# Two value products per unit put into one slot: third and fourth chunk in slot 5 instead of slots 4 and 6

## The chip, the cores and the metric

The kernel runs on one core of a Trainium2 chip. The metric is the time of one execution on the device in microseconds (us). A measurement shows the median of several runs; the profile is of one execution.

The engines named below are TensorE (PE in rows; PEld is its weight load), VectorE (DVE), ScalarE (ACT), GpSimd (POOL) and SyncE (SP), which issues most of the transfers. Each works through its own list of instructions in order and waits on the others only through semaphores.

## What is computed

The first half is attention with normalised queries and keys, the second a mixture of eight experts, of which each token takes one:

```python
q_n, k_n = rmsnorm(q, g_q), rmsnorm(k, g_k)        # (8, 12, 448, 64)
scores = scale * np.matmul(q_n, k_n.transpose(0, 1, 3, 2))
scores = scores - np.max(scores, axis=-1, keepdims=True)
attn = np.exp(scores)
attn = attn / (np.sum(attn, axis=-1, keepdims=True) + 1e-09)
x = np.matmul(attn, v)                             # to (3584, 768)
...
logits = x @ w_gate + modality_bias[modality_id]
e_idx = np.argmax(logits, axis=1)
...
h = np.maximum(x[mask] @ w1[e], 0.0)               # per expert e
out[mask] = gate_w[mask, None] * (h @ w2[e])
```

The change lies in the attention half.

## The kernel before

The 8 batches of 12 heads are worked through in 48 units (`NU`); a unit is two heads of one batch. The 448 positions of each of the two heads are cut into chunks of 128 rows, with one chunk (number 3) that is shared: it holds 64 rows of either head. So a unit has seven row chunks, and the loop gives it seven slots (`NJ = 7`); slot number n = 7 * unit + j is what the table `PLAN` speaks in.

In slot j of unit i the loop issues:

- `st(i, j)`, L1000: the transposed scores of one chunk, two products of 448 columns into PSUM (four in slot 3), and, on ScalarE, the exponential of them into the buffer `p` of the unit. PSUM has two such buffers, so st of a slot needs the exponential of two slots before.
- `sa(u, j)`, L972 and L967: the scores of a unit two further on, the other way round, from which VectorE takes the maximum per row. There are two PSUM buffers here as well: sa of a slot needs the maximum of two slots before to be done.
- what `PLAN` puts there: the transposes of queries and keys (`tr`, slots 0 and 3), of the row maxima (`mt`, slot 1), of the attention output (`xt`, slot 4), the column sums (`sums`, L1054, slot 2 of every second unit), the gate products (`gates`, L1061, slot 6 of every fourth), the matmuls of routing (`rt`, slot 6 of some).
- the value products `av(u, c)`, L1039, of the unit before, u = i - 1, with c from 0 to 3:

```python
for h in range(2):
    j, r = (3, (LO, HI)[h]) if c == 3 else (4 * h + c, slice(0, 128))
    PE.matmul(t["av"][64 * h : 64 * h + 64, :S], lhsT=vv[r, u % 3, j],
              rhs=t["p"][r, j], start=c == 0, stop=c == 3)
```

Chunks 0 to 2 multiply 128 rows by 64 columns for either head; chunk 3 multiplies 64 rows by 64 columns. All four add up in one PSUM tile, of which there is one (`ps_o`). When chunk 3 has been issued, ScalarE copies the tile out with the next slot's first work (`avcopy`), so that chunk 0 of the next unit may begin.

`PLAN['av']` gives the slot of each of the four chunks: `AVJ[c]` in

```python
put(NJ * (u + 1) + (AVJ[c] if u < NU - 2 else min(AVJ[c], 6)), "av", u, c)
...
if c == 3:
    at(pre["A"] if j else post, n + (j > 0), lambda u=u: avcopy(u))
```

Further on, work of routing (small steps of VectorE, GpSimd and ScalarE that decide each token's expert) is mixed into the slots from a queue, a step or two per slot. When the loop ends, the four chunks of the last unit are issued in a row, and the expert half begins.

Of the kernel before, what the change touches and what calls it, by code (L numbers as in the profile page):

```python
# [30 lines left out]
NT1 = NB1 * S  # L31
BIG = float(1 << 20)
ET = mybir.EngineType
PLAN = {'rtj': 6, 'rushat': 36, 'av': (1, 1, 4, 6), 'xt': 4, 'xte': (2, 5), 'sm': 2, 'la': 6, 'rc': 9, 'csv': (1,), 'csj': (3, 6), 'csd': (1, 1), 'cse': (2, 1), 'sa': 14, 'mt': 6, 'tk': 21, 'tq': 18, 'nq': 26, 'nk': 26, 'sk': 49, 'sq': 50, 'rs': 48, 'ld': 58, 'first': {('sq', 0): -22, ('sk', 0): -21, ('nk', 0): -20, ('nq', 0): -18, ('sq', 1): -19, ('sk', 1): -19, ('sq', 2): -18, ('sk', 2): -18, ('nk', 1): -16, ('nq', 1): -13, ('tk', 0): -18, ('tq', 0): -17, ('sa', 0): -15, ('tk', 1): -13, ('tq', 1): -11, ('sa', 1): -5, ('mt', 0): -8, ('tk', 2): -8, ('tq', 2): -3, ('nq', 2): -8, ('nk', 2): -14, ('nq', 3): 3, ('nk', 3): -3, ('sq', 3): -13, ('sk', 3): -13, ('sq', 4): -8, ('sk', 4): -15, ('sq', 6): -2, ('sk', 6): 6, ('sk', 7): 11, ('sq', 8): 5, ('sk', 8): 5, ('nk', 7): 20, ('nq', 9): 31, ('tq', 3): 5, ('mt', 1): 2, ('nq', 5): 6, ('mt', 8): 50, ('rs', 0): -20, ('rs', 2): -16, ('nq', 8): 35, ('rs', 5): -7, ('mt', 2): 8, ('nq', 7): 25, ('mt', 5): 30, ('sk', 9): 15, ('tk', 9): 43, ('mt', 6): 37, ('nq', 6): 17, ('sa', 5): 23, ('rs', 7): 16, ('rs', 8): 30, ('mt', 4): 23, ('nk', 4): -2, ('ld', 9): 6, ('tk', 5): 16, ('sk', 5): -9, ('tk', 3): 0, ('tk', 4): 8, ('nk', 5): 0, ('sq', 5): -15, ('mt', 3): 16, ('nq', 4): 1, ('sa', 4): 16, ('tq', 4): 12, ('sa', 3): 9, ('sa', 2): 1, ('tq', 5): 19, ('mt', 7): 45, ('tq', 7): 31, ('sa', 7): 37, ('nk', 6): 16, ('tq', 6): 24, ('sq', 7): 12, ('tk', 6): 21, ('sa', 6): 30, ('tk', 7): 28}, 'rs0': {0: 0, 2: 1, 5: 0, 7: 0, 8: 2}, 'sastep': 1, 'start': -22, 'warm': {-22: 19, -21: 3, -20: 1, -16: 4, -15: 1, -13: 5, -10: 2, -7: 3, -6: 1, -5: 1, 5: 1, 7: 1}, 'warmn': 1, 'early': 1, 'late0': 1, 'pmp0': 2, 'ramp': 10, 'pmp': (0, 0, 1, 1, 1, 0, 1), 'nv': [(0, 0)], 'pmpa': (1, 0, 1, 0, 1, 1, 1), 'rush': (1, 1, 1), 'ps': [(6, 1), (4, 0), (3, 0), (2, 0)], 'pa': [], 'rtr': 6, 'sml': 4, 'lv': (-10, 0), 'lg': 16, 'lz': 13, 'gc': 24, 's1': (1, 4)}
MANUAL = {ET.PE, ET.DVE, ET.Activation, ET.Pool, ET.SP}
IOFF = bass.IndirectOffsetOnAxis

# [29 lines left out]
def kernel(  # L67
# [727 lines left out]
    if True:  # L795
# [27 lines left out]
        def sumsq(u, i):  # L823
# [4 lines left out]
            sq = sq_b[i]  # L828
            if (u, i) in PLAN["pa"]:
                x = T[u][nm].rearrange("p h c d -> p (h c) d")  # L830
# [9 lines left out]
            def reduce():  # L840
                if (u, i) in PLAN["ps"]:
                    o = t["ss"][:, i, 8 * j : 8 * j + 8].unsqueeze(2)
                    w = D // 2
                    while w:
                        G.tensor_tensor(out=sq[:, :, 0:w] if w > 1 else o, in0=sq[:, :, 0:w],
                                        in1=sq[:, :, w : 2 * w], op=ALU.add)
                        w //= 2
                    return
                V.tensor_reduce(
                    out=t["ss"][:, i, 8 * j : 8 * j + 8], in_=sq, op=ALU.add, axis=AX.X  # L850
                )
# [35 lines left out]
        def tr(u, g):  # L887
# [32 lines left out]

            own = u < PLAN["early"]
            x = ps if own else h_.bitcast(F32)
# [38 lines left out]
        def sa(u, j):  # L961
# [6 lines left out]
            else:  # L968
                h = j // 4
                a = 128 * j - h * S  # L970
                r = slice(0, 128) if u >= PLAN["early"] else (LO, HI)[h]
                PE.matmul(ps[:, :S], lhsT=t["qq"][r, h, a : a + 128], rhs=t["kk"][h][r], start=True, stop=True)  # L972
# [234 lines left out]
        man = ExitStack()  # L1207
        P = PLAN
        man.enter_context(tc.manual_schedule(engines=MANUAL))
# [50 lines left out]
        post, fin = {}, {}  # L1260
        P = PLAN
        CSV, CSJ, CSD, CSE = (P[x] for x in ("csv", "csj", "csd", "cse"))
# [384 lines left out]
```

## Time and profile before

| | |
|---|---|
| median of 3 runs | 1071.11 us (1068.9 to 1071.33) |
| the profiled execution | 1071.33 us |
| its span, first to last instruction | 1069.3 us |
| TensorE busy | 1040.7 us, 97% of the span |
| VectorE busy | 779.2 us, 73% |
| ScalarE busy | 696.2 us, 65% |
| GpSimd busy | 710.3 us, 66% |
| mean granted clock of TensorE | 0.993 |

The table is an average over two halves with different work; the attention loop ends at about 568 us. A share of busy time says which engine has the least room, and not whether its instructions follow each other as closely as they could. That is read from start to start in the timeline.

### The profile page before, as it was taken

What the parts mean: (1) busy time and instruction counts of PE and PEld (TensorE: products, weight loads), DVE (VectorE), ACT (ScalarE), POOL (GpSimd) and SP (SyncE); (2) the same over time, 40 slices, a digit from 0 to 9 for tenths busy, and PEclk for the clock granted to TensorE, in tenths of its full rate; (3) what the DMA queues carried; (4) which work ended last, traced back from release to release, by engine and by line L of the source; (5) the groups of instructions that cost most, each with busy time, mean ns of one, the idle gap of its engine ahead of it and who ended that gap; (6) DMA issues with size and microseconds to landing.
All of it is one profiled execution on the core that took longest, in us unless ns stands there. A gap on an engine that the chain in (4) does not pass through costs nothing.

```text
span 1069.3 us, 19016 instructions
## 1 busy us (share of the span) xinstructions
PE 1040.7 (97%) x6536; PEld 804.7 (75%) x6536; DVE 779.2 (73%) x1337; ACT 696.2 (65%) x1293; POOL 710.3 (66%) x740
## 2 busy tenths in 40 slices
PE   8899999999999999998999999999999999999995
PEld 7555555555555555554557999999999999999995
DVE  5767788998889888898778895856765668556740
ACT  6887888878888788887664654555554555445531
POOL 7788777787877878788875647555445564555451
PEclk9999999999999999999999999999999999999998
DMA  7866767867778678765675704344283432334261
GB/s 188 196 155 147 165 147 188 184 146 162 152 178 188 151 160 155 176 157 118 160 220 188 176 31 118 105 119 115 85 300 93 120 104 76 74 104 119 70 210 50
DMA packets 151800, 153.72 MB, mean 144 GB/s; under 512 B 73530, under 2 KB 141582, under 8 KB 151184
## 3 DMA queue, kind: packets, MB, share of 16 engines
q1 hardware_dynamic: 126340, 110.59, 43.4%
q0 software_dynamic: 25328, 41.82, 12.5%
q8 instruction: 54, 0.88, 0.4%
q14 instruction: 50, 0.41, 0.2%
q10 hardware_dynamic: 28, 0.01, 0.0%
HBM read 150.31 MB, written 33.39 MB: 172 GB/s over the span
## 4 chain that ended last, share of the span: by engine, by line
PE 82%; DVE 5%; POOL 4%; issue 4%; DMA 3%; ACT 2%; SPq 0%; POOLq 0%; DVEq 0%; ACTq 0%
PE ph L591 21%; PE py L621 20%; PE av L1039 12%; PE st L1000 12%; PE sa L972 5%; PE tr L895 3%; PE xt L1096 2%; PE sm L1054 2%; DVE at_hlw L52 2%; POOL r2w L52 1%; PE warm L1249 1%; PE sm L1061 1%; PE mt L983 1%; DVE xw L52 1%; PE sa L967 1%
## 5 line engine op out<-in xcount | busy, mean ns | idle before, releaser
L591 PE MATMUL ph<-xw,w1w 128*128 128x256 f32 x2016 | 246.5, 283 | 1.0 <-ACT xw L52 0.6
L591 PEld LDWEIGHTS ph<-xw,w1w 128*128 128x128 f32 x2016 | 244.0, 192 | 3.4 <-issue 1.4
L52 DVE TENSOR_REDUCE at_hlw<-sa 128x1 f32<-128x448 f32 x336 | 205.6, 617 | 36.4 <-PE sa L972 17.2
L1000 PE MATMUL st<-w1w 128*128 128x448 f32 (+1 forms) x480 | 175.8, 416 | 0.6 <-ACT r2w L52 0.6
L52 ACT ACTIVATE r2w<-st 128x448 f32<-128x448 f32 x168 | 90.8, 543 | 53.2 <-PE st L1000 44.3
L52 POOL TENSOR_TENSOR r2w<-r2w 128x448 f32<-128x448 f32 (+1 forms) x72 | 82.2, 1142 | 63.0 <-ACT at_w2lw L52 22.6
L1000 PEld LDWEIGHTS st<-w1w 128*128 128x128 f32 (+1 forms) x480 | 84.9, 191 | 45.0 <-ACT r2w L52 17.8
L52 POOL DMA_INDIRECT r<-in_moe_w_dram,tb_w x60 | 79.5, 1324 | 58.1 <-DVE w1w L52 42.8
L972 PE MATMUL sa<-w1w 128*128 128x448 f32 (+1 forms) x288 | 110.1, 383 | 8.1 <-DVE at_hlw L52 4.0
L621 PE MATMUL py<-w2lw,hhw 128*128 128x384 f32 x448 | 113.7, 334 | 0.0
L52 ACT ACTIVATE hhw<-ph 128x512 fp32r<-128x512 f32 x56 | 33.5, 598 | 120.6 <-PE ph L591 100.7
L52 DVE TENSOR_TENSOR w1w<-r,w1w 128x768 fp32r<-128x768 f32 x112 | 103.7, 954 | 8.4 <-ACT w1w L52 7.2
L52 ACT CAST w1w<-xw 64x448 fp32r<-64x448 f32 x188 | 105.5, 561 | 3.6 <-issue 1.6
L52 DVE TENSOR_TENSOR w2lw<-r2w,w2ha 128x1536 fp32r<-128x1536 f32 x28 | 49.1, 1757 | 79.1 <-ACT w2ha L52 42.1
L52 POOL DMA_INDIRECT r2w<-in_moe_w_dram,tb_vi x48 | 50.9, 1059 | 83.5 <-DVE w2lw L52 71.6
L52 ACT ACTIVATE at_w2lw<-st 128x448 f32<-128x448 f32 x168 | 90.4, 543 | 23.8 <-PE st L1000 16.8
L1000 PE MATMUL st<-w1w,w2ha 65*128 65x448 f32 x288 | 100.8, 370 | 0.3 <-DMA w1w<-xw 0.3
L52 POOL TENSOR_TENSOR xrw<-r,at_hlw 112x512 f32<-112x512 f32 x95 | 98.1, 1053 | 0.6
L52 ACT CAST w1w<-r 128x768 fp32r<-128x768 f32 x112 | 95.2, 905 | 0.0
L621 PEld LDWEIGHTS py<-w2lw,hhw 128*128 128x128 f32 x448 | 80.9, 188 | 0.0
L52 ACT ACTIVATE yw<-py,ltn 128x384 f32<-128x384 f32 x55 | 29.3, 578 | 77.0 <-PE py L621 48.8
L52 POOL TENSOR_TENSOR r2w<-r2w,at_w2lw 64x448 f32<-64x448 f32 (+1 forms) x48 | 55.0, 1146 | 27.0 <-DVE r2w L52 14.7
(315 smaller groups left out, 2227.1 us busy)
## 6 DMA issues: line engine op xcount, KB each, us to landing
w1w<-xw SPq DMA_DIRECT2D x312, 112.0 KB
xg<-xrw SPq DMA_DIRECT2D x14, 768.0 KB
xrw<-xg SPq DMA_DIRECT2D x56, 192.0 KB
r<-in_q_dram SPq DMA_DIRECT2D x19, 448.0 KB
r<-in_k_dram SPq DMA_DIRECT2D x19, 448.0 KB
w2ha<-xw SPq DMA_DIRECT2D x72, 112.0 KB
r2w<-in_v_dram SPq DMA_DIRECT2D x24, 224.0 KB
at_w2lw<-in_v_dram SPq DMA_DIRECT2D x24, 224.0 KB
```

Of the source, the lines that this page charges most:

```text
L52: return fn(*a, **kw)
L591: PE.matmul(ps[:, i], lhsT=lt_, rhs=rt_[:, c], start=n == 0, stop=n == 17)
L621: PE.matmul(ps[n][:, :384], lhsT=lt_[:, j, 128 * t : 128 * t + 128], rhs=rt_[:, 384 * n : 384 * n + 384], start=j == 0 and m == 0, stop=j ...
L895: PE.transpose(sp[:, c], src[:, c], idn[:CP, :CP])
L967: PE.matmul(ps[:, :S], lhsT=qm_b[u % 2], rhs=hi_b[u % 2][1], start=True, stop=True)
L972: PE.matmul(ps[:, :S], lhsT=t["qq"][r, h, a : a + 128], rhs=t["kk"][h][r], start=True, stop=True)
L983: PE.transpose(ps[0:NJ, :128], t["mx"], idn)
L1000: PE.matmul(ps[:, :S], lhsT=l, rhs=t["qq"][:, h] if first else t["ql"][:, h], start=first and (j != 3 or h == 0), stop=not first and (j != ...
L1039: PE.matmul(t["av"][64 * h : 64 * h + 64, :S], lhsT=vv[r, u % 3, j], rhs=t["p"][r, j], start=c == 0, stop=c == 3)
L1054: PE.matmul(R[g][32 * i : 32 * i + 32, :S], lhsT=sel[:, m], rhs=T[u + i // 2]["cs"][:, i % 2], start=m == 0, stop=False, tile_position=(0, ...
L1061: PE.matmul(sm[32 * i : 32 * i + 32, :S], lhsT=wg[:, (4 * g + i) % NP], rhs=T[4 * g + i]["xt"], start=False, stop=True, tile_position=(0, ...
L1096: PE.transpose(ps[:CP, 128 * c : 128 * c + 128], T[u]["xt"][:, c * CP : (c + 1) * CP], idn)
```

## The change

One entry of the table is changed, the slots of the four value chunks:

```diff
 PLAN = {
 ...
-'av': (1, 1, 4, 6),
+'av': (1, 1, 5, 5),
 ...
```

No instruction is added or removed. On TensorE, in the slots 4 to 6 of an ordinary unit, stood before (a number ending a name is that of the tile; `st_4` is the score tile of slot 4; x2 and x4 are matmuls alike in a row):

```order
L972 MATMUL sa_4_1486<-w1w 128x448
L1039 MATMUL av_1435<-at_w2lw,r2w 64x448 x2
L1096 MATMUL xt_1490<-idn,at_hlw 112x128 x4
L1000 MATMUL st_5_1506<-w1w 128x448
L1000 MATMUL st_5_1506<-w1w,w2ha 128x448
L972 MATMUL sa_5_1509<-w1w 128x448
L1000 MATMUL st_6_1518<-w1w 128x448
L1000 MATMUL st_6_1518<-w1w,w2ha 128x448
L972 MATMUL sa_6_1521<-w1w 128x448
L1039 MATMUL av_1435<-at_w2lw,r2w 64x448 x2
L1000 MATMUL st_0_1530<-w1w 128x448
```

and in the same place stands now:

```order
L972 MATMUL sa_4_1486<-w1w 128x448
L1096 MATMUL xt_1488<-idn,at_hlw 112x128 x4
L1000 MATMUL st_5_1504<-w1w 128x448
L1000 MATMUL st_5_1504<-w1w,w2ha 128x448
L972 MATMUL sa_5_1507<-w1w 128x448
L1039 MATMUL av_1435<-at_w2lw,r2w 64x448 x4
L1000 MATMUL st_6_1520<-w1w 128x448
L1000 MATMUL st_6_1520<-w1w,w2ha 128x448
L972 MATMUL sa_6_1523<-w1w 128x448
L1000 MATMUL st_0_1531<-w1w 128x448
```

The two pairs of value products have moved together behind sa of slot 5; xt follows sa of slot 4 directly, and st of the next unit's slot 0 follows sa of slot 6.

On ScalarE the copy of the value tile goes along. From the exponential of slot 5 to that of the next unit's slot 0 (`xrw<-r` is a square of queries for their norm) stood before, at another unit:

```order
L52 ACTIVATE r2w<-st_5_1023 128x448
L52 ACTIVATE r2w<-st_6_1033 128x448
L52 ACTIVATE xrw<-r_0_152 112x512
L52 COPY at_w2lw<-av_942 128x448
L52 ACTIVATE at_w2lw<-st_0_1045 128x448
```

and now:

```order
L52 ACTIVATE r2w<-st_5_1021 128x448
L52 COPY at_w2lw<-av_942 128x448
L52 ACTIVATE r2w<-st_6_1035 128x448
L52 ACTIVATE xrw<-r_0_152 112x512
L52 ACTIVATE at_w2lw<-st_0_1046 128x448
```

The copy has moved ahead of the exponential of slot 6 and of the square. On VectorE, GpSimd and SyncE the instructions stand in the same order as before.

## Rows read from the trace of the kernel before

**Rows 1.** Windows: length, then busy us of PE, PEld, DVE, ACT, POOL, PEclk, DMA.

```profile
100.00:488.00 388.00, 385.23 (x2088) 221.07 (x2085) 329.00 (x648) 318.96 (x700) 301.39 (x323) 1.00 0.72 163
488.00:515.00 27.00, 24.14 (x122) 12.61 (x120) 24.07 (x55) 15.96 (x35) 21.59 (x29) 0.94 0.48 111
```

**Rows 2.** Timeline of PE, slots 4 to 6 of a unit: start us, us.

```profile
214.24 0.37 PE L972 MATMUL sa<-w1w 128*128 128x448 f32 x1
...
215.44 0.65 PE L1096 MATMUL xt<-idn,at_hhw 128*112 128x128 f32 x4
215.84 0.45 PE L1000 MATMUL st<-w1w 128*128 128x448 f32 x1
...
216.34 0.37 PE L972 MATMUL sa<-w1w 128*128 128x448 f32 x1
...
216.75 0.37 PE L1000 MATMUL st<-w1w,w2ha 65*128 65x448 f32 x1
216.96 0.37 PE L972 MATMUL sa<-w1w 128*128 128x448 f32 x1
217.26 0.97 PE L1039 MATMUL av<-at_w2lw 64*64 64x448 f32 x4
218.16 0.47 PE L1000 MATMUL st<-w1w 128*128 128x448 f32 x1
218.47 0.37 PE L1000 MATMUL st<-w1w,w2ha 65*128 65x448 f32 x1
```

**Rows 3.** Timeline of PE, late unit: xt behind st, no value chunk ahead.

```profile
549.32 0.37 PE L1000 MATMUL st<-w1w,w2ha 65*128 65x448 f32 x1
549.53 0.60 PE L1096 MATMUL xt<-idn,at_hhw 128*112 128x128 f32 x4
549.88 0.64 PE L1000 MATMUL st<-w1w 128*128 128x448 f32 x2
```

**Rows 4.** Timeline of PE: two value chunks in a row, and four.

```profile
219.99 1.72 PE L1039 MATMUL av<-r2w,at_w2lw 128*64 128x448 f32 x8
221.65 0.28 PE L983 MATMUL mt<-idn,at_hlw 128*7 128x128 f32 x1
...
568.14 3.38 PE L1039 MATMUL av<-at_w2lw 128*64 128x448 f32 x16
571.44 0.74 PE L591 MATMUL ph<-xw,w1w 128*128 128x256 f32 x4
```

**Rows 5.** Waits of PE from 40 to 488 us: total, times, longest.

```profile
PE av L1039 <- ACT at_hhw L52: 1.3, 2, 0.9
```

**Rows 6.** Timeline of DVE from slot 5 on, first and last of three units.

```profile
151.48 1.25 DVE L52 TENSOR_REDUCE at_hlw<-sa 128x1 f32<-128x448 f32 x2
152.65 0.89 DVE L53 TENSOR_REDUCE lo<-at_hlw 112x32 f32<-112x384 f32 x1
...
157.12 0.61 DVE L52 TENSOR_REDUCE at_hlw<-sa 128x1 f32<-128x448 f32 x1
...
420.68 0.89 DVE L53 TENSOR_REDUCE lo<-at_hlw 112x32 f32<-112x384 f32 x1
```

**Rows 7.** Timeline of PE: sa of slot 3 in the first of these units.

```profile
157.94 0.37 PE L967 MATMUL sa<-xw,w2ha 128*128 128x448 f32 x1
```

**Rows 8.** Timeline of DVE, a unit with gates and routing: first and last named.

```profile
217.91 1.47 DVE L52 SCALAR_TENSOR_TENSOR r2w<-r2w,half 128x448 f32<-128x448 f32 x1
...
227.08 0.61 DVE L52 TENSOR_REDUCE at_hlw<-sa 128x1 f32<-128x448 f32 x1
```

**Rows 9.** Timeline of PE in the same unit: sa of slot 5, gate products.

```profile
227.74 0.47 PE L972 MATMUL sa<-w1w 128*128 128x448 f32 x1 [0.39 <-DVE at_hlw L52]
...
230.10 0.56 PE L1061 MATMUL sm<-at_hlw,wg 128*32 128x448 f32 x1
```

**Rows 10.** Timeline of POOL: the last addition of a unit's half-sums.

```profile
389.88 1.14 POOL L52 TENSOR_TENSOR at_w2lw<-r2w,at_w2lw 128x448 f32<-128x448 f32 x1
```

**Rows 11.** Timeline of PE: the column sums that read it.

```profile
391.89 0.57 PE L1054 MATMUL sm<-at_hhw,sel 128*32 128x448 f32 x2
```

More of the change, by code (lines that the diff above doesn't have):

```diff
@@ L33 @@
 ET = mybir.EngineType
-PLAN = {'rtj': 6, 'rushat': 36, 'av': (1, 1, 4, 6), 'xt': 4, 'xte': (2, 5), 'sm': 2, 'la': 6, 'rc': 9, 'csv': (1,), 'csj': (3, 6), 'csd': (1, 1), 'cse': (2, 1), 'sa': 14, 'mt': 6, 'tk': 21, 'tq': 18, 'nq': 26, 'nk': 26, 'sk': 49, 'sq': 50, 'rs': 48, 'ld': 58, 'first': {('sq', 0): -22, ('sk', 0): -21, ('nk', 0): -20, ('nq', 0): -18, ('sq', 1): -19, ('sk', 1): -19, ('sq', 2): -18, ('sk', 2): -18, ('nk', 1): -16, ('nq', 1): -13, ('tk', 0): -18, ('tq', 0): -17, ('sa', 0): -15, ('tk', 1): -13, ('tq', 1): -11, ('sa', 1): -5, ('mt', 0): -8, ('tk', 2): -8, ('tq', 2): -3, ('nq', 2): -8, ('nk', 2): -14, ('nq', 3): 3, ('nk', 3): -3, ('sq', 3): -13, ('sk', 3): -13, ('sq', 4): -8, ('sk', 4): -15, ('sq', 6): -2, ('sk', 6): 6, ('sk', 7): 11, ('sq', 8): 5, ('sk', 8): 5, ('nk', 7): 20, ('nq', 9): 31, ('tq', 3): 5, ('mt', 1): 2, ('nq', 5): 6, ('mt', 8): 50, ('rs', 0): -20, ('rs', 2): -16, ('nq', 8): 35, ('rs', 5): -7, ('mt', 2): 8, ('nq', 7): 25, ('mt', 5): 30, ('sk', 9): 15, ('tk', 9): 43, ('mt', 6): 37, ('nq', 6): 17, ('sa', 5): 23, ('rs', 7): 16, ('rs', 8): 30, ('mt', 4): 23, ('nk', 4): -2, ('ld', 9): 6, ('tk', 5): 16, ('sk', 5): -9, ('tk', 3): 0, ('tk', 4): 8, ('nk', 5): 0, ('sq', 5): -15, ('mt', 3): 16, ('nq', 4): 1, ('sa', 4): 16, ('tq', 4): 12, ('sa', 3): 9, ('sa', 2): 1, ('tq', 5): 19, ('mt', 7): 45, ('tq', 7): 31, ('sa', 7): 37, ('nk', 6): 16, ('tq', 6): 24, ('sq', 7): 12, ('tk', 6): 21, ('sa', 6): 30, ('tk', 7): 28}, 'rs0': {0: 0, 2: 1, 5: 0, 7: 0, 8: 2}, 'sastep': 1, 'start': -22, 'warm': {-22: 19, -21: 3, -20: 1, -16: 4, -15: 1, -13: 5, -10: 2, -7: 3, -6: 1, -5: 1, 5: 1, 7: 1}, 'warmn': 1, 'early': 1, 'late0': 1, 'pmp0': 2, 'ramp': 10, 'pmp': (0, 0, 1, 1, 1, 0, 1), 'nv': [(0, 0)], 'pmpa': (1, 0, 1, 0, 1, 1, 1), 'rush': (1, 1, 1), 'ps': [(6, 1), (4, 0), (3, 0), (2, 0)], 'pa': [], 'rtr': 6, 'sml': 4, 'lv': (-10, 0), 'lg': 16, 'lz': 13, 'gc': 24, 's1': (1, 4)}
@@ new lines @@
+PLAN = {'rtj': 6, 'rushat': 36, 'av': (1, 1, 5, 5), 'xt': 4, 'xte': (2, 5), 'sm': 2, 'la': 6, 'rc': 9, 'csv': (1,), 'csj': (3, 6), 'csd': (1, 1), 'cse': (2, 1), 'sa': 14, 'mt': 6, 'tk': 21, 'tq': 18, 'nq': 26, 'nk': 26, 'sk': 49, 'sq': 50, 'rs': 48, 'ld': 58, 'first': {('sq', 0): -22, ('sk', 0): -21, ('nk', 0): -20, ('nq', 0): -18, ('sq', 1): -19, ('sk', 1): -19, ('sq', 2): -18, ('sk', 2): -18, ('nk', 1): -16, ('nq', 1): -13, ('tk', 0): -18, ('tq', 0): -17, ('sa', 0): -15, ('tk', 1): -13, ('tq', 1): -11, ('sa', 1): -5, ('mt', 0): -8, ('tk', 2): -8, ('tq', 2): -3, ('nq', 2): -8, ('nk', 2): -14, ('nq', 3): 3, ('nk', 3): -3, ('sq', 3): -13, ('sk', 3): -13, ('sq', 4): -8, ('sk', 4): -15, ('sq', 6): -2, ('sk', 6): 6, ('sk', 7): 11, ('sq', 8): 5, ('sk', 8): 5, ('nk', 7): 20, ('nq', 9): 31, ('tq', 3): 5, ('mt', 1): 2, ('nq', 5): 6, ('mt', 8): 50, ('rs', 0): -20, ('rs', 2): -16, ('nq', 8): 35, ('rs', 5): -7, ('mt', 2): 8, ('nq', 7): 25, ('mt', 5): 30, ('sk', 9): 15, ('tk', 9): 43, ('mt', 6): 37, ('nq', 6): 17, ('sa', 5): 23, ('rs', 7): 16, ('rs', 8): 30, ('mt', 4): 23, ('nk', 4): -2, ('ld', 9): 6, ('tk', 5): 16, ('sk', 5): -9, ('tk', 3): 0, ('tk', 4): 8, ('nk', 5): 0, ('sq', 5): -15, ('mt', 3): 16, ('nq', 4): 1, ('sa', 4): 16, ('tq', 4): 12, ('sa', 3): 9, ('sa', 2): 1, ('tq', 5): 19, ('mt', 7): 45, ('tq', 7): 31, ('sa', 7): 37, ('nk', 6): 16, ('tq', 6): 24, ('sq', 7): 12, ('tk', 6): 21, ('sa', 6): 30, ('tk', 7): 28}, 'rs0': {0: 0, 2: 1, 5: 0, 7: 0, 8: 2}, 'sastep': 1, 'start': -22, 'warm': {-22: 19, -21: 3, -20: 1, -16: 4, -15: 1, -13: 5, -10: 2, -7: 3, -6: 1, -5: 1, 5: 1, 7: 1}, 'warmn': 1, 'early': 1, 'late0': 1, 'pmp0': 2, 'ramp': 10, 'pmp': (0, 0, 1, 1, 1, 0, 1), 'nv': [(0, 0)], 'pmpa': (1, 0, 1, 0, 1, 1, 1), 'rush': (1, 1, 1), 'ps': [(6, 1), (4, 0), (3, 0), (2, 0)], 'pa': [], 'rtr': 6, 'sml': 4, 'lv': (-10, 0), 'lg': 16, 'lz': 13, 'gc': 24, 's1': (1, 4)}
```

## The prediction

> **What bounds the kernel now.** The table of windows comes first [rows 1]. Between 100 and 488 us, where 35 of the 48 units run, TensorE's matmuls fill 385.23 of 388 us at the full granted clock; VectorE is busy for 329.00 us (85%), so it is the engine that is next. Only in 488 to 515 us does this turn round: VectorE 24.07 of 27 us, TensorE 24.14, the granted clock 0.94. So in most of the loop a change is worth what it changes in TensorE's own sequence, as long as VectorE and ScalarE can still follow.
>
> Busy time can hide a delay between matmuls, so the timeline of one unit is read next, by the distances from start to start [rows 2]. Shown are slots 4 to 6 of an ordinary unit. Matmuls of one kind follow each other at 0.20 to 0.21 us (216.75 to 216.96). A value product (av) after sa starts at 0.30 (216.96 to 217.26); what follows a value chunk starts 0.90 after it (217.26 to 218.16), and the second st after it 0.31 later (218.16 to 218.47) where it is otherwise 0.20. So there is a toll for going into the narrow value products and one for coming out.
>
> **The change part by part: TensorE.** Work is neither added nor removed; the sum is of tolls.
>
> Slot 4 now: from sa to the first st of slot 5 takes 1.60 (214.24 to 215.84), of it 0.40 for the transposes xt (215.44 to 215.84). Without the value chunk, xt follows directly. That occurs once in the trace [rows 3]: 0.21 to get into xt and 0.35 until the next st. So slot 4 will take 0.56, which is 1.04 less.
>
> Slot 6 now: from sa to the second st of the next slot is 1.51 (216.96 to 218.47). Later it will be as from slot 5 to 6 now, 0.41 (216.34 to 216.75). 1.10 less.
>
> Slot 5 now: 0.41. Later: 0.30 into the chunks, the pair, then 0.31. The pair's cost is the question. Two chunks in a row in slot 1 take 1.66 (219.99 to 221.65) [rows 4], so that a second one costs 0.76; by this row the pair takes 1.66. But chunks 0 to 2 are products of 128 rows by 64 columns of the array, and chunk 3 is 64 by 64. The last unit's four chunks in a row take 3.30 (568.14 to 571.44) [rows 4]: three of one shape are 0.90 + 0.76 + 0.76 = 2.42, which leaves 0.88, a full price within rounding, for the fourth. I take this row, since it holds the very pair: 0.90 + 0.90 = 1.80. The Trainium skill, "TensorEngine Tiling (Array Packing)", section Tiling Modes, says that changing the tiling mode, and not just the tile, drains TensorE. The trace agrees: the fourth chunk costs 0.12 us more than one of the same shape. By the rule the pair saves nothing in itself.
>
> By the row of slot 1 alone the gain in an ordinary unit would be 0.28 us, by the row of the last unit it is 0.14, as follows.
>
> Slot 5 will take 0.30 + 1.80 + 0.31 = 2.41, which is 2.00 more. An ordinary unit: -1.04 - 1.10 + 2.00 = -0.14 us; what is left is one toll on the way in (0.09) and the 0.05 by which xt is shorter. There are 22 such units: -3.1. In the others slot 4 or slot 6 has more work of the narrow kind behind the chunk, so its tolls stay and only the chunk's 0.90 goes: 8 units with gate products in slot 6, -1.04 - 0.90 + 2.00 = +0.06 each, +0.5; 6 units with sums in slot 4, -0.90 - 1.10 + 2.00 = 0. In 4 units routing products of the wide kind follow in slot 6, which keep the 0.31 behind them: -1.04 - (0.30 + 0.90 - 0.21 + 0.05) + 2.00 = -0.08, -0.3. The first units have no xt: in four of them slot 4 gives 1.10 as well, -0.2 each, -0.8, of which I count half, since TensorE also waits for others there. The last two give -0.2. Together -3.5.
>
> **ScalarE.** Its one moved step is the copy of av out of PSUM. It now stands before the exponential of slot 6, not behind it. TensorE waited 1.3 us, twice, at av for that copy, in the early units [rows 5]. These waits go, less what the sums behind them then wait for: -0.8. The price: ScalarE is in order, so the exponential of slot 6 is held until av is done. But its own input comes after av on TensorE, so it loses only the copy. I cost this at nothing. The cover is slot 0: the st of slot 1 is the next that needs that exponential, and between lie two st, one sa and four transposes, some 0.6 + 0.35 us by the rows of their kinds [rows 2, 3]. Were the cover gone, that st would be late by up to the length of the copy in each unit.
>
> **VectorE, where the loss lies.** The order on VectorE, GpSimd and the DMA queues is the same before and after. But TensorE's slots change in length. sa of slot 5 comes 1.04 earlier; sa of slot 6 comes later by -1.04 + (0.30 + 1.80) - 0.21 + (0.31 - 0.20) = +0.96, I use 0.94 for the rounding; what follows in slot 0 is 0.15 earlier again. VectorE's maximum over sa of slot 6 moves with it, by 0.94, where VectorE does not lag, and all behind it (the half-sums, the sums of squares, the maximum of slot 0) has 0.94 + 0.15 = 1.09 less time until TensorE wants the buffer back: sa of slot 3 needs the maximum of slot 1. In an ordinary unit VectorE has idle time in slots 0 to 3 that takes this up. In units in which routing work is mixed in it has none:
>
> - Three units are like [rows 6]: from 151.48 VectorE runs on without a gap, through two routing steps (0.89 the first), to the maximum at 157.12, done 157.73. TensorE starts sa of slot 3 at 157.94 [rows 7], so 0.21 are in hand. After: done 158.67, wanted at 157.79: a wait of 0.88. The last of the three, at 420.68, reads the same; the middle one has 0.2 more in hand. Together 2.5.
> - Two units are like [rows 8]: VectorE runs without a gap from 217.91, and a routing step delays it again before the maximum of slot 3 (227.08 to 227.61). Today sa of slot 5 waits for that (227.74) and the chunk of slot 6 is done when the gate sums start at 230.10 [rows 9]. After: the maximum is done at 228.55 and sa starts at 228.68; then 0.30 + 1.80 + 0.31 + 0.21 to sa of slot 6 and 0.30 to the sums: 231.60, 1.5 later. Together about 3.1, with what the unit would have given.
> - Four units, in which VectorE now lags by more than 0.8 when slot 6 ends, hand on TensorE's earlier start only as a wait: 0.5 in all, an estimate.
>
> **GpSimd.** It adds the half-sums up from VectorE's step behind the maximum of slot 6, so it too is 0.94 late. In every second unit the column sums of slot 2 need it: 391.02 against 391.89 [rows 10, 11], 0.87 in hand, 1.09 needed: 0.3 with the signal; two others have just enough, 0.1 each. 0.5.
>
> What is not in the trace is whether VectorE's small steps change in length when they fall beside other work of GpSimd; they run from 0.17 to over 2 us. I bound the waits by this: none of them comes (0), or as much again comes in the routing units (13); I take the sum above, 6.6, since each term is read from its own rows.
>
> **The sum.** -3.5 - 0.8 + 6.6 = +2.3 us, on the profiled execution's 1071.33, of which 1069.3 is its span: 1073.6. That execution lies 0.2 above the median, so 1073.4 is to be compared with it; I put it at 1073. At the two ends of the waits the same sum gives 1066.8 and 1080.
>
> **The rivals.**
> 1. *The waits don't come*, because VectorE makes the 0.94 good. Then -3.5 - 0.8 = -4.3: about 1066.8. For it: VectorE has 59 us idle in 388 [rows 1], 1.7 per unit, more than 0.94. Against: in the five units named its rows have no gap.
> 2. *VectorE and ScalarE fall behind in ordinary units too.* The place is sa of slot 3 after a short slot 2. There the trace has some 0.8 in hand in the tightest units without sums, of which ScalarE's later copy takes about 0.3. It decides from 0.5 more per unit; each 0.3 beyond that costs 22 x 0.3 = 6.6, so 1073 + 6 = 1079. For it: three short slots, 6, 0 and 2, now lie around one long one. Against: VectorE's gaps there. This ends slower.
> 3. *The shape change is not paid*, the pair at 1.66: 40 x 0.14 = 5.6 less, 1067.4. Against it stands the row of four chunks.
> 4. *The stretch at 488 to 515 decides.* There TensorE waits for VectorE, which waits for GpSimd, and the clock fell; if that wait shortens or lengthens by 2 us, the time moves by 2 to 4 us either way: 1069 to 1077. The order there is unchanged, so I expect the same stall.
>
> **How the numbers follow.** The sum as worked out 0.54, the first rival 0.17, the second 0.13, the third 0.03, the fourth 0.13. 0.3% of 1071.11 is 3.2 us, about what a measurement can tell: faster is below 1067.9, slower above 1074.3. My own case by itself reaches from 1070.5 to 1075.5, so it gives 0.36 same and 0.18 slower; rivals 1 and 3 are faster but for 0.02; rival 2 is slower; rival 4 is split 0.07 same, 0.02 faster, 0.04 slower. Together faster 0.20, same 0.45, slower 0.35. For 8 in 10 the range takes in rival 1 down to its own value and leaves out the far part of rival 2: 1066.8 to 1077.5.
>
> **What the profile after would show.** av in slot 5 as one group of eight records with 1.80 from its start to st 6, not 1.66; ordinary units 0.14 shorter; no wait of av for ScalarE's copy; waits of sa of slot 3 for VectorE of 0.8 or more near 158, 292 and 426 us, and a longer unit near 218 and 353; VectorE idle about 1.4 us before the maximum of slot 6 in ordinary units. I am wrong if the waits of sa for VectorE stay at some 2 us between 100 and 488, or if they appear in ordinary units as well.

## The result and the profile after

The changed kernel takes 1076.92 us (median of 15 runs, 1073.05 to 1081.97), the kernel before 1071.40 in the same session (15 runs, 1068.89 to 1075.15): a ratio of 1.0053, 95% interval 1.0037 to 1.0069, so 4.0 to 7.4 us slower. The forecast was 1073, its range 1066.8 to 1077.5. The profiled execution is the longest of its 15, 1081.97 us with a span of 1080.0, while the profile of before (1071.33) lies close to its median. So it has to be read unit by unit, and what only this execution met has to be told apart.

The table of windows, with the columns of [rows 1]:

```profile
100.00:488.00 388.00, 377.71 (x2043) 219.04 (x2043) 317.28 (x631) 310.29 (x687) 296.10 (x314) 0.99 0.72 162
488.00:515.00 27.00, 25.91 (x139) 14.40 (x136) 24.25 (x58) 18.84 (x43) 20.98 (x30) 1.00 0.52 120
```

TensorE has 7.5 us less busy time in the long stretch (377.71 for 385.23). The short one, rival 4's place, can't be compared so: the changed kernel is 9.8 us behind by then and does other work in it. It is judged by its units further on. The timeline of TensorE in slots 4 to 6 of a unit, against [rows 2]:

```profile
272.80 0.37 PE L972 MATMUL sa<-w1w 128*128 128x448 f32 x1
273.00 0.60 PE L1096 MATMUL xt<-idn,at_hhw 128*112 128x128 f32 x4
273.36 0.45 PE L1000 MATMUL st<-w1w 128*128 128x448 f32 x1
273.64 0.37 PE L1000 MATMUL st<-w1w,w2ha 65*128 65x448 f32 x1
273.86 0.37 PE L972 MATMUL sa<-w1w 128*128 128x448 f32 x1
274.16 1.87 PE L1039 MATMUL av<-r2w 128*64 128x448 f32 x8
275.96 0.47 PE L1000 MATMUL st<-w1w 128*128 128x448 f32 x1
276.27 0.37 PE L1000 MATMUL st<-w1w,w2ha 65*128 65x448 f32 x1
276.48 0.37 PE L972 MATMUL sa<-w1w 128*128 128x448 f32 x1
```

The pair costs 1.80 from its start to the next st (274.16 to 275.96), the toll behind it is 0.31, and slot 4 is down to 0.56 (272.80 to 273.36). VectorE idles ahead of the maximum of slot 6, as forecast:

```profile
276.89 0.62 DVE L52 TENSOR_REDUCE at_hlw<-sa 128x1 f32<-128x448 f32 x1 [1.47 <-PE sa L972]
```

Waits of TensorE from 40 to 500 us: total, times, longest. No wait of av for ScalarE's copy is left, against [rows 5]:

```profile
PE sa L972 <- DVE at_hlw L52: 5.8, 7, 1.4
PE mt L983 <- DVE at_hlw L52: 3.1, 3, 2.0
PE st L1000 <- DMA w1w<-xw: 3.0, 1, 3.0
PE sa L967 <- DVE at_hlw L52: 1.7, 4, 0.4
```

L967 is sa of slot 3. Before, the two lines of sa had 1.7 and 0.9. Of the 5.8, one wait of 1.34 is put down to VectorE wrongly:

```profile
279.70 0.44 PE L972 MATMUL sa<-w1w 128*128 128x448 f32 x1 [1.34 <-DVE at_hlw L52]
```

VectorE's last maximum ahead of it, the one at 276.89 shown above, was done by 277.51. What came just before the start is the end of a copy into w1w: it was issued at 273.35, and the last of its 16 completions in the trace stands at 279.61. So the waits at sa of L972 for VectorE are 4.5 us, and this one belongs to the late transfers below.

A finer measure serves for all that follows: the start of sa of slot 0 in each unit, here less the same start before. From one unit to the next this difference moves by -0.15 or -0.16 in ordinary units and by 0.08 in units with gates. It moves by about +0.9 in five units with routing (those that begin at 153, 219, 288, 353 and 421 us before; 0.80 at 288, and the last measured as 0.91 where only the later units are changed, since here a late transfer lies on it). VectorE in the first of these, against [rows 6]:

```profile
155.35 0.62 DVE L52 TENSOR_REDUCE at_hlw<-sa 128x1 f32<-128x448 f32 x1 [1.47 <-PE sa L972]
155.90 0.90 DVE L53 TENSOR_REDUCE lo<-at_hlw 112x32 f32<-112x384 f32 x1
...
157.87 0.84 DVE L53 TENSOR_TENSOR lo<-lo,ball 112x32 f32<-112x32 f32 x1
158.64 0.61 DVE L52 TENSOR_REDUCE at_hlw<-sa 128x1 f32<-128x448 f32 x1
...
160.36 0.61 DVE L52 TENSOR_REDUCE at_hlw<-sa 128x1 f32<-128x448 f32 x1
```

It first waits 1.47 for sa of slot 6, then runs two routing steps without a gap. TensorE pays for it in two places: by the starts against before, 0.26 at sa of slot 2 and the rest, 0.68, at sa of slot 3 [rows 7]:

```profile
159.31 0.47 PE L972 MATMUL sa<-w1w 128*128 128x448 f32 x1
...
161.02 0.47 PE L967 MATMUL sa<-xw,w2ha 128*128 128x448 f32 x1 [0.44 <-DVE at_hlw L52]
```

Two things were not foreseen. The first is an early unit (it begins at 67 us), in which mt waits 1.96 for VectorE, where it waited 0.92 before, and the granted clock then stands at the lower of its two levels (1.2 GHz, half) from 69.31 to 72.73. The unit is 2.36 longer. First before, then after:

```profile
68.52 0.28 PE L983 MATMUL mt<-idn,at_hlw 128*7 128x128 f32 x1 [0.92 <-DVE at_hlw L52]
```
```profile
67.14 0.37 PE L972 MATMUL sa<-w1w 128*128 128x448 f32 x1
69.47 0.38 PE L983 MATMUL mt<-idn,at_hlw 128*7 128x128 f32 x1 [1.96 <-DVE at_hlw L52]
69.50 1.84 PE L1000 MATMUL st<-w1w 128*128 128x448 f32 x4
```

The second are late transfers: copies of queries and keys from one half of the partitions to the other (w1w from xw, 112 KB each). The longest:

```profile
429.48 0.47 PE L1000 MATMUL st<-w1w 65*128 65x448 f32 x1 [2.97 <-DMA w1w<-xw]
```

This wait and the one at 279.70 were each followed by another fall of the granted clock to half, at 431.13 and 280.94.

### The profile page after: what moved, and what is told of

Same layout as the page of the kernel before. It is cut to its first block, busy times and chain, and to the rows that moved or that the text cites. A ratio compares the mean times of both kernels' runs of the same rounds, so it can differ in the third digit from the quotient of the medians.

```text
span 1080.0 us, 19016 instructions
## 1 busy us (share of the span) xinstructions
PE 1042.0 (96%) x6536; PEld 808.5 (75%) x6536; DVE 773.3 (72%) x1337; ACT 694.4 (64%) x1293; POOL 704.1 (65%) x740
## 4 chain that ended last, share of the span: by engine, by line
PE 76%; DVE 7%; DMA 6%; issue 5%; POOL 3%; ACT 3%; SPq 0%; POOLq 0%; DVEq 0%; ACTq 0%
PE ph L591 20%; PE py L621 18%; PE av L1039 12%; PE st L1000 12%; PE sa L972 4%; DMA w1w<-xw 3%; PE tr L895 3%; DVE at_hlw L52 3%; PE sm L1054 2%; PE xt L1096 1%; PE warm L1249 1%; DVE xw L52 1%; POOL r2w L52 1%; PE sa L967 1%; ACT xw L52 1%
## 5 line engine op out<-in xcount | busy, mean ns | idle before, releaser
L1000 PE MATMUL st<-w1w 128*128 128x448 f32 (+1 forms) x480 | 178.7, 421 | 4.9 <-DMA w1w<-xw 3.0
L972 PE MATMUL sa<-w1w 128*128 128x448 f32 (+1 forms) x288 | 109.8, 382 | 12.9 <-DVE at_hlw L52 9.8
```

Of the source, the lines that this page charges most:

```text
L1000: PE.matmul(ps[:, :S], lhsT=l, rhs=t["qq"][:, h] if first else t["ql"][:, h], start=first and (j != 3 or h == 0), stop=not first and (j != ...
```

## The experiments

Each experiment was timed against the kernel before in the same session on the same chip; there before's median was 1072.07 (the first four rows of the table below the change), 1071.02 (the next four) and 1075.80 us (the last four). Theory 1: VectorE is late behind sa of slot 6, which comes 0.94 later. Theory 2: the pair itself costs TensorE. Theory 3: late transfers and falls of the clock, met by chance.

The accounts come from one profile of each kernel, as differences to the profile of before. "Early" is what the units from 56 to 110 us lose, "loop" what the units from 110 to 536 us lose, without six (they begin at 265, 276, 399, 410, 421 and 525 us before) in which the kernels met most of their late transfers; these six have a column of their own, which holds 0.9 of a routing unit too. In the kernel with chunk 2 in slot 1 the clock fell at 54 us, just ahead of the early units, so its -0.88 there is no gain. An account is one execution and not the median: the profiles of the change and of the kernel with the transposes first are the longest of their runs, those of the pair in slot 6 and of the pair in all but eight are the fastest.

| kernel | early | loop | the six | ratio, 95% interval |
|---|---|---|---|---|
| the change | +2.24 | -0.11 | +7.79 | 1.0053, 1.0037 to 1.0069 |
| pair in the first units only | +1.07 | -0.51 | +4.45 | 1.0011, 0.9991 to 1.0031 |
| pair in the later units only | +0.03 | -0.29 | +3.54 | 1.0026, 1.0000 to 1.0053 |
| chunk 3 alone to slot 5 | +1.32 | +0.73 | +2.58 | 1.0046, 1.0022 to 1.0070 |
| chunk 2 alone to slot 5 | +0.26 | +2.00 | +3.19 | 1.0039, 1.0016 to 1.0062 |
| pair in slot 6 | +0.17 | +3.05 | -1.39 | 1.0049, 1.0028 to 1.0070 |
| change, routing step in slot 5 | +2.26 | -1.47 | +4.51 | 1.0013, 0.9996 to 1.0030 |
| chunk 2 third in slot 1 | -0.88 | +3.77 | +4.01 | 1.0070, 1.0046 to 1.0094 |
| pair in 18 ordinary units | +0.01 | -3.72 | +3.29 | 0.9971, 0.9956 to 0.9987 |
| before, routing step in slot 5 | +0.03 | -1.38 | +7.39 | 0.9987, 0.9957 to 1.0016 |
| change, transposes first | +0.93 | +0.11 | +11.91 | 1.0022, 1.0003 to 1.0041 |
| pair in all but eight, step moved | +0.01 | -2.89 | +2.81 | 1.0016, 0.9990 to 1.0041 |
| mixed | +0.02 | -4.83 | +6.90 | 0.9993, 0.9968 to 1.0018 |

**Half of the change each: the first units, then the later ones.**

```diff
-put(NJ * (u + 1) + (AVJ[c] if u < NU - 2 else min(AVJ[c], 6)), "av", u, c)
+put(NJ * (u + 1) + ((AVJ if u + 1 < 7 else (1, 1, 4, 6))[c]), "av", u, c)
```

> The pair in slot 5 only in the first six units, the other units as before. Theory 1 (VectorE is late behind sa of slot 6): the early units show a cost of their own, since the transposes of the row maxima (mt) wait for VectorE there: +2 us, 1073.4, with the wait of mt near 69 us at about 1.9 instead of 0.9. Theory 2 (the pair itself costs TensorE more in every unit): six of 47 units, +0.7 us, 1072. Theory 3 (the time was lost to transfers that came late by chance and to falls of the clock, wherever the chunks stand): no change, 1071.4.

The later ones, with `u + 1 >= 7` in its place:

> The pair in slot 5 only from the seventh unit on, the first units as before. Theory 1: waits of sa for VectorE in five units with routing (near 159, 223 to 228, 296, 360 to 365, 427 us), together some 5 to 6 us, against 3 us saved in the ordinary units: +3 us, 1074.4. Theory 2: 41 of 47 units, +5 us, 1076, with ordinary units longer than before. Theory 3: 1071.4.

Medians 1074.03 and 1075.29. Each half keeps its part: with the pair in the first units mt waits 1.96 again, with the pair in the later ones the early units stay as before and the routing units lose 0.91, 0.94, 0.47, 0.90 and 0.91. The two medians lie 2.0 and 3.2 above before's, 5.2 together, near the loss of the whole change; but the first one's interval takes in no change, so how the time divides is not shown. What the traces show is that the early units, in which a gain was forecast, lose.

**One chunk moved at a time.**

```diff
-'av': (1, 1, 5, 5),
+'av': (1, 1, 4, 5),
```

> Chunk 2 stays in slot 4, chunk 3 alone goes from slot 6 to slot 5: no pair, the same number of ways into and out of the narrow products. Theory 1: sa of slot 6 is 1.1 us late and sa of slot 0 is where it was, so VectorE has 1.1 us less, as in the change; the same waits (6 to 7 us) but no saving: +6 us, 1077.5. Theory 2: no pair, so no change, 1071.4.

And chunk 2 alone, `'av': (1, 1, 5, 6)`:

> Chunk 3 stays in slot 6, chunk 2 alone goes from slot 4 to slot 5. Theory 1: sa of slot 6 keeps its place (+0.06), so VectorE is not late; TensorE pays 0.06 more in each unit with an xt in slot 4 (its own way into the narrow products comes on top of nothing saved): +2 us, 1073.5, and the waits of sa for VectorE between 100 and 488 us stay at some 2 us. Theory 2: no pair, so no change, 1071.4.

Medians 1077.97 and 1077.08. Chunk 3 alone in slot 5, without any pair, brings the early wait (mt 1.85) and the losses of the units at 153, 288 and 421 us (1.01, 0.40 and 0.92), so these come from what slot 5 holds ahead of slot 6, not from the pair. The two units with gates and routing, at 219 and 353, lose nothing by it (-0.45 and -0.46). With chunk 2 alone, sa of slot 6 comes at about its old time: mt waits as before, and the early loss and that of the three units are gone. Instead sa of slot 5, which now comes earlier, meets VectorE in the two units with gates and routing, and these lose 0.63 and 0.61:

```profile
67.55 0.28 PE L983 MATMUL mt<-idn,at_hlw 128*7 128x128 f32 x1 [0.92 <-DVE at_hlw L52]
```
```profile
227.36 0.47 PE L972 MATMUL sa<-w1w 128*128 128x448 f32 x1 [1.43 <-DVE at_hlw L52]
```

Ordinary units changed by 0.00 and +0.05, so neither chunk by itself saves a toll. Both kernels are slower without a pair, so theory 2 is not needed for a loss. But chunk 2 alone was expected at 1073.5 and came out 5.0 above before's median, of which its account has 2.3 outside the six: that was a miss.

**The pair in slot 6.**

```diff
-'av': (1, 1, 5, 5),
+'av': (1, 1, 6, 6),
```

> The pair as it is, but in slot 6 instead of slot 5. Theory 1 (the loss is that sa of slot 6 comes 0.94 later, with VectorE's maximum behind it): here sa of slot 6 comes about 1.04 earlier than before, so the steps of +0.9 in the units with routing (those that begin at 140, 280 and 410 us) are gone; the ordinary unit keeps its -0.14 to -0.16, and from the unit at 110 to the one at 500 the time is 2 to 4 us less than before, apart from waits of sa of slots 5 and 6 for VectorE, which has less time in slots 4 and 5. Total about 1069 to 1071 where before is 1071.5. Theory 2 (the pair itself, wherever it stands, costs TensorE or the clock time): as the change, 1075 to 1078. Theory 3 (late transfers and clock falls that a kernel meets by chance make up the loss): the steps of the units as in theory 1, and the total anywhere from 1069 to 1077.

Median 1077.02, where 1069 to 1071 was expected: no better than the change, so theory 1 as I had put it is too narrow. The early wait and the routing waits did go (mt now 0.40), and ordinary units keep their -0.14 to -0.16. But sa of slot 5 comes a chunk earlier in every unit, and TensorE waits for VectorE there. Its waits from 40 to 500 us:

```profile
PE sa L972 <- DVE at_hlw L52: 9.3, 12, 1.2
PE mt L983 <- DVE at_hlw L52: 1.0, 3, 0.4
```

That is 9.3 us where before had 1.7 and the change 4.5. It is the spreading of the chunks, between slots 4 and 6, that gave VectorE its time; a pair in every unit, in slot 5 or in slot 6, takes it away somewhere. This profile is the fastest of its 12 (1072.37): its account gives +1.8 in all, and the rest of the median's loss is not traced.

**The routing step moved to slot 5, in the changed kernel and in before.** `pmp` has, for each slot, how many steps of the routing queue may be issued in it behind VectorE's maximum.

```diff
-'pmp': (0, 0, 1, 1, 1, 0, 1),
+'pmp': (0, 0, 1, 1, 1, 1, 0),
```

> The changed kernel, with the routing step that stands behind sa of slot 6 in VectorE's order moved to slot 5, where the pair now runs and VectorE has idle time. The work is the same. Theory 1: the waits of sa of slot 3 for VectorE near 159, 296 and 427 us become shorter than 0.3, and these units lose less than 0.2 against before instead of 0.9; the total is 2 to 3 us under that of the change, about 1074. Theory 2: nothing changes but those waits' place; 1076 to 1078. Theory 3: the waits go, but the total moves by less than a measurement can tell.

> The kernel before with the routing step moved to slot 5, as in the experiment on the change. Theory 1 (the moved step only takes away waits that the change brought): in before that step has no such wait, so the total stays within 1 us of before's, 1070 to 1072. Against it (the step's place is a gain of its own, 3 to 4 us, whatever the value products do): 1067 to 1068.

The change with the moved step has 1072.59: 1.0013 instead of 1.0053, so 4.3 us less (give or take 2.5, the two intervals taken together). The step now fills VectorE's idle time ahead of sa of slot 6, which shrinks from 1.47 to 0.72, and sa of slot 3 follows st without a wait:

```profile
153.55 0.83 DVE L53 TENSOR_REDUCE lo<-at_hlw 112x32 f32<-112x384 f32 x1
155.10 0.62 DVE L52 TENSOR_REDUCE at_hlw<-sa 128x1 f32<-128x448 f32 x1 [0.72 <-PE sa L972]
```
```profile
159.01 0.98 PE L1000 MATMUL st<-w1w 128*128 128x448 f32 x4
159.95 0.47 PE L967 MATMUL sa<-xw,w2ha 128*128 128x448 f32 x1
```

That unit now moves by +0.08 instead of +0.91, the one at 288 us by 0.00, the one at 421 by -0.04; the two at 219 and 353 keep 0.84 and 0.75, since there the step that counts is another, of 2.69 us ahead of the maximum that sa of slot 5 needs. In the change:

```profile
227.10 2.69 DVE L53 TENSOR_TENSOR oh<-i_e,ei 112x32 f32<-112x32 f32 x1
```
```profile
230.38 0.48 PE L972 MATMUL sa<-w1w 128*128 128x448 f32 x1 [1.43 <-DVE at_hlw L52]
```

In before the moved step gives 1.4 in the loop, most of it in the units around 219 and 353, and a ratio that shows no difference. So theory 1 holds for the three units: the same work, in the time that the pair left idle, costs nothing.

**Three chunks of one shape in a run.**

```diff
-'av': (1, 1, 5, 5),
+'av': (1, 1, 1, 6),
```

> Another pair: chunk 2, which has the shape of chunks 0 and 1, goes to slot 1 as the third of a run, and chunk 3 alone to slot 6. By the rows of before a run of three of one shape costs 0.90 + 0.76 + 0.76, and slot 4 loses 1.04, so an ordinary unit is 0.28 shorter, twice what the pair gives. Theory 1: sa of slot 2 comes 0.76 later and sa of slot 5 1.04 earlier, sa of slot 6 and all behind it as before but 0.28 earlier; VectorE has to make the maxima of slots 4 to 6 in less time, so in the units with routing, where it runs without a gap, 3 to 6 us of waits come back out of 22 x 0.28 + 14 x 0.14 = 8. Total 1066 to 1070. Theory 2 (what counts is a change of shape): -0.28 in each ordinary unit, 1064 to 1066. Theory 3: as theory 1 for the units' steps, the total 2 to 4 above that.

Median 1079.85, the slowest. The sum of tolls was right: the run takes 2.41 (0.90 + 0.76 + 0.76 = 2.42 was worked out), and ordinary units without a wait are 0.29 to 0.30 shorter.

```profile
133.61 2.48 PE L1039 MATMUL av<-r2w 128*64 128x448 f32 x12
136.02 0.28 PE L983 MATMUL mt<-idn,at_hlw 128*7 128x128 f32 x1
```
```profile
PE sa L972 <- DVE at_hlw L52: 10.0, 15, 1.4
```

But the waits for VectorE from 40 to 500 us rise to 10.0. The miss is the same as with the pair in slot 6: I had counted 3 to 6.

**The pair only where VectorE has time.**

```diff
-put(NJ * (u + 1) + (AVJ[c] if u < NU - 2 else min(AVJ[c], 6)), "av", u, c)
+put(NJ * (u + 1) + ((AVJ if u + 1 in (7, 8, 11, 12, 14, 15, 18, 19, 20, 23, 24, 26,
+    27, 30, 31, 32, 35, 36) else (1, 1, 4, 6))[c]), "av", u, c)
```

> The pair only in 18 ordinary units whose neighbours have no routing and no sums; all others as before. Theory 1: the gain of 0.15 in these units stays (-2.7) and no wait for VectorE is added: 1068.5 to 1069.5 where before is 1071.5, and the waits of TensorE at sa are those of before within 0.5. Theory 2: the total is at or above before's. Theory 3: the units' steps as in theory 1, and the total between 1068 and 1073 with no sign of its own.

Median 1068.77 against 1071.02, ratio 0.9971, interval 0.9956 to 0.9987: faster than before, by what the tolls give (2.7 worked out; by the ratio 1.4 to 4.7). Waits at sa for VectorE are 2.0 us from 40 to 500, where before has 1.7:

```profile
PE sa L972 <- DVE at_hlw L52: 2.0, 6, 0.5
```

So the pair itself is a gain, where VectorE can follow; theory 2 falls.

**The transposes ahead of the pair in two early units.** In these units the transposes of query rows stand in slot 5, behind the pair.

```diff
+for a in todo.get("tr", ()) if n < 49 and j == 5 else ():
+    a0, a1, a2, d_ = tr(*a)
+    ...
 for u, c in todo.get("av", ()):
     av(u, c)
 ...
-for a in todo.get("tr", ()):
+for a in todo.get("tr", ()) if n >= 49 or j != 5 else ():
```

> The changed kernel; in slot 5 of the two early units that have transposes of query rows there, these transposes stand ahead of the pair on TensorE, and on ScalarE the cast of them ahead of the copy of av. Nothing else moves. Theory 4 (the early loss: the transposes and their cast wait behind the pair and its copy, and all of ScalarE's and VectorE's queue behind them is late): the wait of mt near 68 to 69 us falls from 1.96 to about 0.9, as before, and the unit that begins at 67 is 1.0 shorter or more; the total is 1 to 2 us under that of the change. Against it (VectorE late behind sa of slot 6, as in the later units): mt waits as long as with the change, and the total stays.

Median 1078.54 against 1075.80: 1.0022, less than the change's 1.0053, but the two intervals overlap. By the trace theory 4 fell: mt waits 1.98, as with the change. ScalarE's timeline says why; first the exponential of slot 6 in before, then this kernel:

```profile
61.90 0.54 ACT L52 ACTIVATE r2w<-st 128x448 f32<-128x448 f32 x1
```
```profile
61.12 0.54 ACT L52 CAST xw<-tr 128x448 fp32r<-128x448 f32 x1
62.39 0.53 ACT L52 COPY at_hhw<-av 128x448 f32<-128x448 f32 x1 [0.72 <-PE av L1039]
63.05 0.55 ACT L52 ACTIVATE r2w<-st 128x448 f32<-128x448 f32 x1
```
```profile
67.38 0.69 DVE L52 SCALAR_TENSOR_TENSOR xw<-tr,gs,xw 128x448 fp32r<-128x448 f32 x1 [1.05 <-ACT xw L52]
```
```profile
69.25 0.28 PE L983 MATMUL mt<-idn,at_hlw 128*7 128x128 f32 x1 [1.98 <-DVE at_hlw L52]
```

The cast is early now, but ScalarE still idles 0.72 for the pair, and the exponential of slot 6 starts at 63.05, since its st stands behind the pair; before it started at 61.90 with the unit at the same place within 0.3. From there ScalarE runs almost without a gap. VectorE waits for it (1.05 at 67.38), and the maxima that mt reads are late with it: mt starts at 69.25, before at 68.52. So it is not VectorE that is late by itself here; the cause is again what stands ahead of slot 6, but through ScalarE. With chunk 2 alone in slot 5, and with the pair in slot 6, st of slot 6 is not late, and the loss was not there: that fits.

**Everything late taken out.** The pair in all units but the first six and the two at 219 and 353 us (these are the ones that the diff takes out; the expectation names the starts of the units just ahead of them), with the moved step:

```diff
-put(NJ * (u + 1) + (AVJ[c] if u < NU - 2 else min(AVJ[c], 6)), "av", u, c)
+put(NJ * (u + 1) + ((AVJ if u + 1 > 6 and u + 1 not in (17, 29) else (1, 1, 4, 6))[c]), "av", u, c)
```

> The pair in all units but the first six and the two that VectorE reaches late (they begin at 208 and 342 us), with the routing step in slot 5. If the loss is all in the early units, in the waits behind sa of slot 6 in the routing units and in these two units, then taking these away leaves the gain of the tolls: -0.15 in 22 units and the small terms, together -3: 1068 where before is 1071. If late transfers or the clock make up the loss, 1070 to 1073.

And with `(1, 1, 1, 6)` in nine of these units (`u + 1` of 7 to 10, 19, 20, 23, 31, 32):

> As the one with the pair in all but eight units and the moved step, but in nine units in which VectorE has idle time chunk 2 goes third in slot 1 and chunk 3 alone to slot 6. By the steps of the kernel that did so everywhere this gives -0.30 in such a unit instead of -0.15, 1.35 more in all: 1066.5 where before is 1071. If VectorE is late after these units too, one or two waits of 0.5 to 1 eat it: 1068.

In the traces both do what was worked out: 2.9 and 4.8 us less in the loop, with steps of -0.29 to -0.31 in the first four units of the second. In time they do not: 1076.85 and 1074.80 against 1075.80, ratios that span no change, where gains of 3 and 4.5 us were expected. Either the gain was lost in transfers, or it is hidden by them: in that session before itself ran from 1070.68 to 1085.39. This is not settled.

**The transfers.** The kernel of before with the moved step has the order of before on TensorE and SyncE, and on ScalarE but for two places (at 217 and 352 us), and yet lost 7.39 us in the six units. The one with the pair in the first units only has the order of before on every engine from 110 us on, and lost 4.45 there. Windows from 400 to 432 us, of before and then of the one with the moved step (columns as in [rows 1]), and where TensorE waited in it:

```profile
400.00:432.00 32.00, 32.00 (x177) 18.62 (x175) 26.47 (x52) 27.32 (x61) 27.21 (x30) 1.00 0.80 152
```
```profile
400.00:432.00 32.00, 29.19 (x148) 15.99 (x146) 22.00 (x42) 23.23 (x50) 25.37 (x27) 0.95 0.84 141
```
```profile
412.64 0.44 PE L972 MATMUL sa<-w1w 128*128 128x448 f32 x1 [0.43 <-issue]
...
424.81 0.47 PE L1000 MATMUL st<-w1w 65*128 65x448 f32 x1 [0.71 <-DMA w1w<-xw]
...
426.85 0.44 PE L972 MATMUL sa<-w1w 128*128 128x448 f32 x1 [1.57 <-DMA w1w<-xw]
```

The DMA engines are busier (0.84 for 0.80) and move less (141 GB/s for 152). At sa of slot 0 of the unit at 276 us (279.70 in the change) the profile often names no releaser; in before and in the kernel with the pair in 18 units:

```profile
276.16 0.44 PE L972 MATMUL sa<-w1w 128*128 128x448 f32 x1 [0.26 <-issue]
```
```profile
276.93 0.44 PE L972 MATMUL sa<-w1w 128*128 128x448 f32 x1 [2.00 <-issue]
```

Here too the last completion of a copy into w1w stands just ahead of the start, at 276.07 and 276.84. That is theory 3: real, several us in a run, and there without the change. Before's own profile met almost none of it, and it lies close to the median of its 15 runs. So how much of it an ordinary execution of before meets, and whether one of the changed kernel meets more, is open.

## Why the prediction was near, and where it was wrong

- **The tolls of TensorE: right.** The pair takes 1.80 (not 1.66), ordinary units lose 0.15 to 0.16 (0.14 worked out), gate units gain 0.08 (0.06). The run of three at 2.41 adds the counterpart: of one shape the second and third chunk cost 0.76 each, of another shape the full 0.90. Rival 3 falls. The Trainium skill, "TensorEngine Tiling (Array Packing)", section Tiling Modes, says that a change of mode drains TensorE; the two prices agree with it.
- **VectorE behind sa of slot 6: right in three units, the term too large in two.** Five units lose 0.9 each, 4.5, where 6.6 was counted with GpSimd. Three of them read 0.91, 0.80 and 0.91 for 0.88. The two with gates and routing lose 0.95 and 0.92 in the balance, not 1.5. There VectorE was to be 0.94 late, and it is 0.3: sa of slots 2 to 5 come 0.28 to 0.30 later in these units. The rest of their loss has the other cause that the prediction counted, the pair behind an sa of slot 5 that waits: chunk 2 alone in slot 5 gives 0.63 and 0.61 there, chunk 3 alone a gain. No other unit of the loop outside the six loses more than 0.13, so the four others (0.5) and GpSimd's term (0.5) can't be made out. Besides, four units give 0.36 to 0.56, more than an ordinary one. In the loop the change costs +0.8 (-0.11 and the 0.91 of the unit at 421), not +3.5. Rival 1, that the waits don't come, fails in the five units.
- **The early units: wrong in sign.** I counted -0.8 for the waits of av and -0.4 for tolls. The waits of av went (the first, at 53 us, gave way to one of 0.66 at sa for VectorE), but the units lose 1.07 in the profile without a fall of the clock and 2.24 with one. The step that failed is "I cost this at nothing": I asked only whether the next st would find its exponential done. I did not follow ScalarE's queue behind the held exponential, which in the early units is full and feeds VectorE and, by it, mt.
- **The sum.** -1.2 and +3.5 were forecast, +1.1 to +2.2 and +0.8 measured: +1.9 to +3.0 for +2.3. Two errors cancel. The median is 5.5 higher, at least 4.0 by its interval. That the traced part comes out near the forecast is luck. The rest, 1.0 to 5.5, lies in late transfers and clock falls if the accounts are complete; the prediction has no term for them. That the changed kernel meets more of them than before is not shown, and the two last kernels, whose accounts promised more than their times gave, leave the same question. So of the 4.0 to 7.4 us only 1.9 to 3.0 have a cause that the traces show.
- **Rivals 2 and 4** did not come: no waits in ordinary units with the pair in slot 5, and the two units that begin at 488 and 500 us in before move by +0.02 and -0.32.

The chances put most on no change; it came out slower, and inside the range.

## What to carry to other kernels

In this kernel a saving on the fullest engine counted only where the next engines could follow: the pair saves 0.15 in each ordinary unit, and used in 18 chosen units it made the kernel faster (0.9971), used in all it made it slower (1.0053). When work is gathered into one slot, list for every engine what the following slots now receive later or earlier, and follow each queue to the next place where the bounding engine waits, in the fullest units first and in the first units too. And where an engine then idles, small work can be moved into that gap: one routing step moved took back 2.3 us in the trace (1.36 in the loop, 0.95 in the unit at 421).

## What was not expected of the hardware

- After TensorE's wait of 1.96 to 1.98 at mt, the granted clock fell to the lower of its two levels (1.2 GHz, half) in two profiles (the change at 69.31, the moved step at 70.73) and not in two others (pair in the first units only, transposes first). From 66 to 76 us its mean was 0.83 and 0.83, against 1.00 and 1.00. The unit lost 2.36 and 2.40 with the fall, 0.86 and 0.87 without.
- Nearly the same program order (one step of VectorE moved) met transfers that moved 7% less from 400 to 432 us (141 for 152 GB/s) with the DMA engines busier, and waited several us for copies of 112 KB. The last of the 16 completions of a copy can come long after the others: for the one issued at 273.35 in the change they run from 275.78 to 279.61.
- A wait can be named wrongly in a profile: the 1.34 at 279.70, put down to VectorE, ended with that copy.
